# Second chunk pair decoded among the attention's last tiles, three products of the first slot behind its transposes, and the last slot and last token tiles reordered

## The chip, the cores and the metric

The kernel runs on one core of a Trainium2 chip. The metric is the device time of one execution in microseconds (us). Engines: TensorE (PE, with its weight loads as PEld), VectorE (DVE), ScalarE (ACT), GpSimd (POOL) and SyncE (SP), whose queue issues nearly all transfers.

## The reference

Three stages follow one another; everything is float32.

```python
scores = (q @ k.T) / sqrt(64) ; decay = cum[:, None] - cum[None, :]   # cum = cumsum(log(clip(f, 1e-4, 1)))
attn = softmax(where(causal, -1e9, scores + decay))                   # 4 batches, 8 heads, 576 tokens, 64 wide
x = (attn @ v)  as [2304 tokens, 512]
h = x @ w_in0  ; x = (h - tanh(h)) @ w_out0      # w_in 512 x 2048, w_out 2048 x 512
h = x @ w_in1  ; out = (h * sigmoid(h)) @ w_out1
```

## The kernel before, in words

**Precision.** Every float32 operand of a product is split in a high and a low part of the TensorE's faster 32-bit type, and each product is three matmuls: high x high, high x low, low x high. The split is a cast (ScalarE) and a subtraction (VectorE). The weights of the two feed-forward layers come as 64-bit words and are decoded on the chip: scale (ScalarE), shift, exponent, low, join (VectorE), then hi (ScalarE) and lo (VectorE). The function `wjob` issues one such step.

**Attention.** `attention` walks through 16 pairs of heads (NP) with 9 score tiles each (NTILE), so N = 144 tiles in all. One step of its loop issues, for tile n, the scores, transposes and values that are due (`later`, `run`), the copies out of PSUM (`evac`), the exponential of tile n - 1 (`expo`), the row minimum of tile n (`least`) and, every third step, the sums and the normalisation (GpSimd) of three tiles. `ahead` holds other work that is issued at the end of a step, by its number relative to N: `at(n - N, ...)`. Transposes have three PSUM tiles (ps_t), the scores four PSUM banks (ps_s), which become the product banks (ps_h) from step N on.

**Feed-forward units.** The hidden columns of a layer are cut into 16 chunks, two of them a pair (q); two pairs form a set. A unit u is (layer, set, block of 768 tokens); there are 24 and each has two slots (j = 0, 1), one for each pair of the set, so NSL = 48 slots. In a slot the first product (x with w_in) is done by a seven-product scheme (`product`, numbered 1 to 7) on blocks of half the width: operands 4 to 7 are made from differences of token blocks (`xtemp`, then `xmake`: cast on ScalarE, subtraction on VectorE, a spill to memory by SP), weights from sums and differences (`sum`). VectorE adds each product from its PSUM bank to half tiles hs (line 379); ScalarE copies product 1. `bend` applies tanh or silu, `high` and `low` split the result, and `project` (line 314) multiplies a half (h) of the tokens' hidden values with w_out.

**Order.** The whole order is written by hand (`tc.manual_schedule`): each engine's queue runs in the order in which the program issues, and a queue whose first instruction waits holds all behind it. `slot_steps` is a generator: a slot is a list of pieces, P for a product and G for one call of `project`; after each piece the items of `xplan` (operands of the next unit) and a share of `fills` (decoding) are issued. The G of slot sl are the projections from number n0 = 8 (sl - 1) - 6 on, so they lag behind their hidden values, and slot 0 has none that does anything. `rest` issues the split of the second half that the slot left over.

Before the change, the steps N - 1 to N + 7 hold the differences and operands of unit 0, steps N + 8 to N + 16 scale to sums of the w_in of pair 1 (`jobs(1, 0, ...)`), and the parts hi and lo of it are fills of slot 0, as is scale to join of w_out of pair 1. Its hi and lo are fills of slot 1, the lo in the last piece; the first projection that needs them is the third of slot 2, number 4 (the projections 0 to 3 belong to pair 0).

**The end.** `halves` lists the projections: per unit, half h, pair j, chunk i, and token group g. In layer 1 the group g = 0 has two tiles of 128 tokens (six matmuls of 512 columns), g = 1 one (three). The last projection of each group ends in an add into an output tile `ob` (line 334) and its transfer (line 336):

```python
ob = wtmp.tile([P, 2, DM], F32, tag="wb", name=f"ob{u}_{h}_{g}")
ob = ob[:, 0:2 - g]
nc.vector.tensor_tensor(ob.rearrange("p t (k w) -> p k t w", w=256), acc, total, ALU.add)
t0 += 256 * g
nc.sync.dma_start(out=out[t0:t0 + P * (2 - g), :].rearrange("(t p) d -> p t d", p=P), in_=ob)
```

The pool wtmp has one buffer for each of its tags wa, wb and ws; wa and wb are also the intermediate tiles of the decoding. The accumulators (ps_a) have two buffers.

Of the kernel before, what the change touches and what calls it, by code (L numbers as in the profile page):

```python
# [7 lines left out]
F32 = mybir.dt.float32  # L8
# [6 lines left out]
P = 128  # L15
# [24 lines left out]
def forgetting_attention_two_ffn(  # L40
# [160 lines left out]
    def jobs(q, m, *lists):  # L201
        return [(q, m) + j for js in lists for j in js] if q < 2 * NPR else []

    fills, late = {}, set()
    for s in range(2 * NSET):
# [11 lines left out]
            fills.setdefault(k + d, []).extend(js)  # L217
        late.add(k + 7)
        fills.setdefault(k + 7, []).extend(jobs(o, 1, LAST))
    fills[0] = jobs(1, 0, HILO) + jobs(1, 1, [("scale",)], PRE)  # L220
    fills[1] = jobs(1, 1, LAST)

    def fill(j):
# [43 lines left out]
    def xat(sl, p, fn, *a):  # L267
        xplan.setdefault((sl, p), []).append((fn, a))
# [3 lines left out]
    for u, (l, s, b) in enumerate(units):  # L272
        if u == 0:
            continue
        if s == 0:
            xat(2 * u - 2, 5, xtemp, l, b, 1)
            xat(2 * u - 2, 6, xtemp, l, b, 2)
            for p, i in ((2, 1), (4, 6), (6, 2)):
                xat(2 * u - 1, p, xmake, u, i)
            xat(2 * u - 1, 7, xtemp, l, b, 4)  # L280
            xat(2 * u - 1, 11, xmake, u, 5)
            xat(2 * u - 1, 12, xtemp, l, b, 3)
            xat(2 * u - 1, 13, xmake, u, 7)
            xat(2 * u, 0, xmake, u, 4)
            xat(2 * u, 2, xmake, u, 3)
        else:
            for i, p in PIECE.items():
                xat(2 * u - 1, p, xload, u, i)

    halves = [(u, h, q, i, g) for u in range(len(units)) for h in range(2) for q in range(2)  # L290
              for i in (1, 0) for g in range(2)]
    gfree, gt, accs, hs = list(range(4)), {}, {}, {}

    def project(n):

        u, h, j, i, g = halves[n]
        l, s, b = units[u]
        gh, gl, slot = gt[u, j, h]
        woh, wol = (w[:, i] for w in wtiles[2 * (u // NB) + j, 1])
        first, last = j == 0 and i == 1, j == 1 and i == 0  # L300
        if first:
            accs[u, h, g] = pools["ps_a"].tile([P, 2, 512], F32, tag="a", name=f"a{u}_{h}_{g}")
        acc = accs[u, h, g]
        ks = range(2) if l == 0 or g == 0 else range(1)
        for k in ks:
            js = slice((2 * g + k) * P, (2 * g + k) * P + P)
            if l == 0:
                terms = ((woh[:, js], gh[:, i]), (woh[:, js], gl[:, i]), (wol[:, js], gh[:, i]))
                dst = acc[:, k, 0:TH]
            else:  # L310
                terms = ((gh[:, i, js], woh), (gh[:, i, js], wol), (gl[:, i, js], woh))
                dst = acc[:, k]
            for r, (w, m) in enumerate(terms):
                nc.tensor.matmul(dst, w, m, start=first and r == 0, stop=last and r == 2)  # L314
        if g == 1 and i == 0:
            gfree.append(slot)
        if not last:
            return
        del accs[u, h, g]
        t0 = TB * b + TH * h  # L320
        if l == 0:
            total, acc = x[:, 2 * g:2 * g + 2, t0:t0 + TH], acc[:, :, 0:TH]
        else:
            total = x[:, 2 * h:2 * h + 2, TB * b + 512 * g:TB * b + 512 * g + (512, 256)[g]]
            total = total.rearrange("p k (t w) -> p k t w", w=256)
            acc = acc[:, 0:2 - g].rearrange("p t (k w) -> p k t w", w=256)
        if s == 0:
            nc.scalar.copy(total, acc)  # L328
        elif l == 0 or s + 1 < NSET:
            nc.vector.tensor_tensor(total, acc, total, ALU.add)  # L330
        else:
            ob = wtmp.tile([P, 2, DM], F32, tag="wb", name=f"ob{u}_{h}_{g}")
            ob = ob[:, 0:2 - g]
            nc.vector.tensor_tensor(ob.rearrange("p t (k w) -> p k t w", w=256), acc, total, ALU.add)  # L334
            t0 += 256 * g
            nc.sync.dma_start(out=out[t0:t0 + P * (2 - g), :].rearrange("(t p) d -> p t d", p=P), in_=ob)
# [12 lines left out]
    def half_tile(u, j, h):  # L349
        hs[h] = pools["hp"].tile([P, 2, TH], F32, tag=f"h{h}", name=f"hs{u}_{j}_{h}")  # L350
        return hs[h]
# [26 lines left out]
    def add(to, p, s):  # L378
        nc.vector.tensor_tensor(to, p, s, ALU.add)  # L379

    def slot_steps(sl):

        u, j = divmod(sl, 2)
        pieces = "P1 G P6 G P2 G G P7 G P5 G P4 G P3 G".split()
        n0 = 8 * (sl - 1) - 6
        todo = list(fills.get(sl, []))
        hooks = [4, 5, 6, 7, 11, 12, 14] if sl in late else [1, 2, 3, 4, 5, 6, 7, 11, 12, 14]
        share = {p: (len(todo) * k // len(hooks), len(todo) * (k + 1) // len(hooks)) for k, p in enumerate(hooks)}
        g = 0
        for p, what in enumerate(pieces):  # L390
            if what == "G":
                if n0 + g >= 0:
                    project(n0 + g)
                g += 1
            else:
                i = int(what[1])
                dst = product(u, j, i)
                if i == 1:
                    nc.scalar.copy(half_tile(u, j, 0)[:, 1], dst)
                    rest()  # L400
                elif i == 6:
                    add(half_tile(u, j, 1)[:, 0], dst, hs[0][:, 1])
                elif i == 2:
                    add(hs[0][:, 1], dst, hs[0][:, 1])
                elif i == 7:
                    add(hs[0][:, 0], dst, hs[1][:, 0])
                elif i == 5:
                    add(hs[1][:, 1], dst, hs[1][:, 0])
                    add(hs[1][:, 0], dst, hs[0][:, 0])
                elif i == 4:  # L410
                    add(hs[0][:, 0], dst, hs[0][:, 0])
                    bend(u, j, 0)
                else:
                    add(hs[1][:, 1], dst, hs[1][:, 1])
                    high(u, j, 0)
                    low(u, j, 0)
                    bend(u, j, 1)
                    left.extend([(high, (u, j, 1)), (low, (u, j, 1))])
            for fn, a in xplan.get((sl, p), []):
                fn(*a)  # L420
            for job in todo[slice(*share.get(p, (0, 0)))]:
                fill(job)
            yield

    def attention():
        with ExitStack() as actx:


# [316 lines left out]

            def open_early():
                early.close()
                open_pools(("ps_h", 4), xb=1)

            ahead = {-12: [(open_earlier,)], 0: [(open_early,)]}  # L750

            def at(n, *item):
                ahead.setdefault(n, []).append(item)
# [10 lines left out]
                at(NTILE * (4 + k // 3) + (1, 3, 5)[k % 3] - N, wjob, *job)  # L764
            for n, i in ((-11, 1), (-8, 2)):
                at(n, xmake, 0, i, nc.gpsimd)
            for n, k in ((-1, 1), (0, 2), (2, 4), (4, 3)):
                at(n, xtemp, 0, 0, k)
            for n, i in ((1, 6), (3, 5), (5, 7), (6, 4), (7, 3)):
                at(n, xmake, 0, i)  # L770
            for k, job in enumerate(jobs(1, 0, [("scale",)], PRE, SUMS)):
                at(8 + k, fill, job)
            for n in range(N + 2 * NTILE):
                if n % NTILE == 0:
                    run(n, scores)
                    run(n, transposes)
                    run(n, values)
                else:
                    run(n, transposes)
                    run(n, values)  # L780
                    run(n, scores)
                if n < NTILE - 1:
                    busy(kqs[0][:, 0], 2)
                run(n, evac)
                if has(n - 1):
                    expo(n - 1)
                run(n, collect)
                if n % 3 == 2 and has(n - 5):
                    guard(n - 5)
                if has(n):  # L790
                    least(tiles[n])
                if n % 3 == 2 and has(n - 5):
                    normalise(n - 5)
                run(n, load_kq, load_v, split, place_last, place_dec, place_dec_last)
                for fn, *a in ahead.get(n - N, []):
                    fn(*a)
        open_pools(("ps_a", 2), hp=1, tp=1, gp=1, wp1=1, wp2=1)
        wpool.update({1: pools["wp1"], 2: pools["wp2"]})

    with tc.manual_schedule():  # L800
        attention()
        for sl in range(NSL):
            for _ in slot_steps(sl):
                pass
        rest()
        for n in range(8 * (NSL - 2) + 2, len(halves)):
            project(n)
# [39 lines left out]
```

## Time and profile before

| | |
|---|---|
| median of 3 runs | 976.05 us (975.76 to 976.42) |
| profiled execution, its own time | 972.9 us |
| its span, first to last instruction | 971.1 us |
| mean granted TensorE clock | 0.989 |
| busy in the span: PE, PEld, DVE, ACT, POOL | 96%, 87%, 76%, 45%, 17% |
| moved by DMA | 188.86 MB, mean 194 GB/s |

The attention ends near 180 us (its last values product starts at 177.49); from there on slots follow each other. GpSimd is busy in the attention alone. Rows of a timeline or of the chain begin with the start and the duration in us; in brackets stands how long the engine was idle before, and what ended that.

### The profile page before, as it was taken

The numbers are of one execution on the slowest core, as the hardware profiler recorded it, in microseconds if no ns is written. First come the engines' busy times: TensorE is split into PE (matmuls) and PEld (weight loads), VectorE is DVE, ScalarE is ACT, GpSimd is POOL, SyncE is SP. The second block draws the span as 40 slices with busy tenths as digits, with TensorE's granted clock in tenths as the row PEclk, the third lists the DMA queues.
The fourth block names the chain that finished last, engine by engine and source line by source line (L and its number), as shares of the span: only waits on it lengthen the run. The fifth ranks groups of instructions, "written<-read, shape, count | busy, mean of one in ns | idle before, by whom it ended". The sixth has DMA issues, their size and how long they took to land.

```text
span 971.1 us, 14858 instructions
## 1 busy us (share of the span) xinstructions
PE 935.5 (96%) x5496; PEld 848.0 (87%) x5496; DVE 740.0 (76%) x1338; ACT 436.4 (45%) x782; POOL 160.5 (17%) x242
## 2 busy tenths in 40 slices
PE   8999999779999999999999989899999999999996
PEld 6777776669999999999999989798898989899884
DVE  7788887899888887888788988785676677765442
ACT  6788888454554333332423354554432334231210
POOL 8999998100000000000000000000000000000000
PEclk9999999899999999999999999999999999999998
DMA  5443343545558564866467345474865477435711
GB/s 163 144 139 121 128 154 122 206 186 222 225 224 312 189 224 138 308 245 207 154 251 271 141 169 234 167 269 166 295 236 191 178 250 271 154 135 189 271 62 68
DMA packets 45800, 188.86 MB, mean 194 GB/s; under 512 B 9440, under 2 KB 9440, under 8 KB 45696
## 3 DMA queue, kind: packets, MB, share of 16 engines
q1 hardware_dynamic: 45720, 187.90, 53.6%
q8 instruction: 43, 0.70, 0.3%
q14 instruction: 29, 0.24, 0.1%
q10 hardware_dynamic: 8, 0.02, 0.0%
HBM read 148.44 MB, written 38.34 MB: 192 GB/s over the span
## 4 chain that ended last, share of the span: by engine, by line
PE 82%; DVE 10%; ACT 3%; issue 2%; POOL 1%; DMA 1%; POOLq 0%; DVEq 0%; ACTq 0%
PE a L314 35%; PE h L346 30%; PE t L594 5%; PE s L547 4%; PE out_t L650 4%; DVE hs L379 3%; PE s L539 2%; PE out_t L678 1%; DVE xt L242 1%; DVE xo L256 1%; ACT t L356 1%; DMA out<-ob 1%; DVE wl L194 1%; DVE t L358 1%; DVE ob L334 1%
## 5 line engine op out<-in xcount | busy, mean ns | idle before, releaser
L346 PE MATMUL h<-xo,wh 128*128 128x384 f32 x1344 | 345.9, 338 | 8.0 <-DVE hs L379 8.0
L346 PEld LDWEIGHTS h<-xo,wh 128*128 128x128 f32 x1344 | 247.8, 190 | 24.2 <-DVE hs L379 7.5
L379 DVE TENSOR_TENSOR hs<-h,hs 128x384 f32<-128x384 f32 x336 | 185.3, 553 | 84.7 <-PE h L346 80.3
L356 ACT ACTIVATE t<-hs 128x768 f32<-128x768 f32 x96 | 81.3, 847 | 355.3 <-DVE hs L379 355.3
L346 PE MATMUL h<-xo,wl 128*128 128x384 f32 x672 | 226.8, 337 | 0.0
L314 PE MATMUL a<-gh,wh 128*128 128x384 f32 x384 | 129.4, 337 | 4.5 <-DVE x L330 4.5
L314 PE MATMUL a<-gh,wl 128*128 128x384 f32 x384 | 129.4, 337 | 2.6 <-DVE wl L194 2.6
L314 PE MATMUL a<-gl,wh 128*128 128x384 f32 x384 | 129.3, 337 | 0.0
L346 PEld LDWEIGHTS h<-xo,wl 128*128 128x128 f32 x672 | 127.3, 189 | 0.0
L369 DVE TENSOR_TENSOR gl<-t,gh 128x768 fp32r<-128x768 f32 x96 | 91.5, 953 | 41.9 <-ACT gh L365 41.7
L314 PE MATMUL a<-wh,gh 128*128 128x512 f32 x288 | 112.8, 392 | 6.4 <-ACT x L328 3.5
L314 PE MATMUL a<-wh,gl 128*128 128x512 f32 x288 | 114.6, 398 | 0.0
L314 PE MATMUL a<-wl,gh 128*128 128x512 f32 x288 | 114.1, 396 | 0.0
L365 ACT CAST gh<-t 128x768 fp32r<-128x768 f32 x96 | 80.4, 837 | 29.5 <-DVE t L358 28.3
L568 ACT ACTIVATE p<-p,mn 128x128 f32<-128x128 f32 (+3 forms) x128 | 71.1, 557 | 14.7 <-DVE mn L560 12.7
L314 PEld LDWEIGHTS a<-gh,wh 128*128 128x128 f32 x384 | 72.5, 189 | 5.4 <-DVE x L330 5.4
L314 PEld LDWEIGHTS a<-gh,wl 128*128 128x128 f32 x384 | 72.7, 189 | 2.9 <-DVE wl L194 2.9
L560 DVE CUSTOM_DVE_ANT_0 p<-s,mask 128x128 f32<-128x128 f32 (+3 forms) x128 | 59.4, 480 | 20.0 <-PE s L547 20.0
L582 POOL TENSOR_SCALAR p<-p,sm 128x128 f32<-128x128 f32 (+3 forms) x128 | 71.8, 580 | 12.6 <-DVE sm L579 8.1
L314 PEld LDWEIGHTS a<-gl,wh 128*128 128x128 f32 x384 | 72.6, 189 | 0.2 <-DVE gl L369 0.2
L314 PEld LDWEIGHTS a<-wh,gh 128*128 128x128 f32 x288 | 54.2, 188 | 14.1 <-DVE ob L334 4.1
L358 DVE TENSOR_TENSOR t<-hs,t 128x768 f32<-128x768 f32 x48 | 46.0, 957 | 25.6 <-ACT t L356 23.6
(90 smaller groups left out, 1233.2 us busy)
## 6 DMA issues: line engine op xcount, KB each, us to landing
xo<-xd SPq DMA_DIRECT2D x126, 768.0 KB
xd<-xo SPq DMA_DIRECT2D x42, 768.0 KB
raw<-w_in SPq DMA_DIRECT2D x32, 512.0 KB
raw<-w_out SPq DMA_DIRECT2D x32, 512.0 KB
kqraw<-kq SPq DMA_DIRECT2D x16, 608.0 KB
vraw<-v SPq DMA_DIRECT2D x16, 320.0 KB
out<-ob SPq DMA_DIRECT2D x6, 512.0 KB
out<-ob SPq DMA_DIRECT2D x6, 256.0 KB
```

Of the source, the lines that this page charges most:

```text
L314: nc.tensor.matmul(dst, w, m, start=first and r == 0, stop=last and r == 2)
L346: nc.tensor.matmul(dst, w[:, ks], m[:, k], start=k == 0 and r == 0, stop=k == 1 and r == 2)
L356: nc.scalar.activation(t, hs[h], AF.Silu if l else AF.Tanh)
L358: nc.vector.tensor_tensor(t, hs[h], t, ALU.subtract)
L365: nc.scalar.copy(gh, hs[h])
L369: nc.vector.tensor_tensor(gl, hs[h], rd(gh), ALU.subtract)
L379: nc.vector.tensor_tensor(to, p, s, ALU.add)
L547: nc.tensor.matmul(s[:, h, c:c + n], a[half(h), q], b[half(h), 0:n], start=r == 0, stop=r == 3,)
L560: nc.vector.tensor_tensor_reduce(out=pt.rearrange("p (g c) -> p g c", g=2) if i == 4 else pt, in0=src, in1=m, op0=ALU.add, op1=ALU.min, sc ...
L568: nc.scalar.activation(pt, pt, AF.Exp, bias=mn, scale=-1.0, accum_out=sums[:, n // 3 % 5, n % 3, 0:1],)
L582: nc.gpsimd.tensor_scalar(pt, pt, sm[:, j:j + 1], 1.0, ALU.mult, ALU.mult)
L594: nc.tensor.transpose(t[:, k], pt[:, c * P:c * P + P], ident)
```

## The change

In the attention, the steps N - 3 to N + 3 get scale, shift, exponent, low and join of pair 1's w_in, one each at N - 3, N - 2, N - 1, N and N + 3; the sums follow at N + 6. The differences and the operands 6, 5, 7 of unit 0 move to steps N + 1 to N + 8. The generator of slot 0 is advanced within the attention, three pieces at the steps N + 3, N + 4 and N + 6: products 1, 2 and 6 of slot 0. The loop ends nine steps earlier; behind it hi and lo of pair 1's w_in are issued, with the operands 4 and 3 of unit 0 in between. In slot 0 product 1 is kept in the second half tile; the five decoding steps of pair 1's w_out stand behind products 7, 5, 4 and two empty G. Unit 1's two first differences move from slot 0 to slot 1, and its operand 1 is made one piece earlier.

At the end, slot 47 runs product 3 before its last two projections and issues the left-over split at once; the last eight projections run with all of g = 0 first; and output tiles of g = 1 take the tag wa.

```diff
@@ -217,7 +217,7 @@
             fills.setdefault(k + d, []).extend(js)
         late.add(k + 7)
         fills.setdefault(k + 7, []).extend(jobs(o, 1, LAST))
-    fills[0] = jobs(1, 0, HILO) + jobs(1, 1, [("scale",)], PRE)
+    fills[0] = jobs(1, 1, [("scale",)], PRE)
     fills[1] = jobs(1, 1, LAST)
 
     def fill(j):
@@ -273,9 +273,10 @@
         if u == 0:
             continue
         if s == 0:
-            xat(2 * u - 2, 5, xtemp, l, b, 1)
-            xat(2 * u - 2, 6, xtemp, l, b, 2)
-            for p, i in ((2, 1), (4, 6), (6, 2)):
+            early = u == 1
+            xat(2 * u - 2 + early, 5 - 3 * early, xtemp, l, b, 1)
+            xat(2 * u - 2 + early, 6 - 3 * early, xtemp, l, b, 2)
+            for p, i in ((2 - early, 1), (4, 6), (6, 2)):
                 xat(2 * u - 1, p, xmake, u, i)
             xat(2 * u - 1, 7, xtemp, l, b, 4)
             xat(2 * u - 1, 11, xmake, u, 5)
@@ -289,6 +290,7 @@
 
     halves = [(u, h, q, i, g) for u in range(len(units)) for h in range(2) for q in range(2)
               for i in (1, 0) for g in range(2)]
+    halves[-8:] = sorted(halves[-8:], key=lambda t: t[4])
     gfree, gt, accs, hs = list(range(4)), {}, {}, {}
 
     def project(n):
@@ -312,7 +314,7 @@
                 dst = acc[:, k]
             for r, (w, m) in enumerate(terms):
                 nc.tensor.matmul(dst, w, m, start=first and r == 0, stop=last and r == 2)
-        if g == 1 and i == 0:
+        if g == 1 and i == 0 and (u, h) != (len(units) - 1, 1):
             gfree.append(slot)
         if not last:
             return
@@ -329,7 +331,7 @@
         elif l == 0 or s + 1 < NSET:
             nc.vector.tensor_tensor(total, acc, total, ALU.add)
         else:
-            ob = wtmp.tile([P, 2, DM], F32, tag="wb", name=f"ob{u}_{h}_{g}")
+            ob = wtmp.tile([P, 2, DM], F32, tag=("wb", "wa")[g], name=f"ob{u}_{h}_{g}")
             ob = ob[:, 0:2 - g]
             nc.vector.tensor_tensor(ob.rearrange("p t (k w) -> p k t w", w=256), acc, total, ALU.add)
             t0 += 256 * g
@@ -382,10 +384,16 @@
 
         u, j = divmod(sl, 2)
         pieces = "P1 G P6 G P2 G G P7 G P5 G P4 G P3 G".split()
+        if sl == 0:
+            pieces = "P1 P2 P6 G G G G P7 G P5 G P4 G P3 G".split()
+        elif sl == NSL - 1:
+            pieces = "P1 G P6 G P2 G G P7 G P5 G P4 P3 G G".split()
         n0 = 8 * (sl - 1) - 6
         todo = list(fills.get(sl, []))
         hooks = [4, 5, 6, 7, 11, 12, 14] if sl in late else [1, 2, 3, 4, 5, 6, 7, 11, 12, 14]
         share = {p: (len(todo) * k // len(hooks), len(todo) * (k + 1) // len(hooks)) for k, p in enumerate(hooks)}
+        if sl == 0:
+            share = {p: (k, k + 1) for k, p in enumerate((7, 9, 10, 11, 12))}
         g = 0
         for p, what in enumerate(pieces):
             if what == "G":
@@ -396,12 +404,16 @@
                 i = int(what[1])
                 dst = product(u, j, i)
                 if i == 1:
-                    nc.scalar.copy(half_tile(u, j, 0)[:, 1], dst)
+                    half_tile(u, j, 0)
+                    p1 = (half_tile(u, j, 1) if sl == 0 else hs[0])[:, 1]
+                    nc.scalar.copy(p1, dst)
                     rest()
                 elif i == 6:
-                    add(half_tile(u, j, 1)[:, 0], dst, hs[0][:, 1])
+                    if sl:
+                        half_tile(u, j, 1)
+                    add(hs[1][:, 0], dst, p1)
                 elif i == 2:
-                    add(hs[0][:, 1], dst, hs[0][:, 1])
+                    add(hs[0][:, 1], dst, p1)
                 elif i == 7:
                     add(hs[0][:, 0], dst, hs[1][:, 0])
                 elif i == 5:
@@ -416,13 +428,15 @@
                     low(u, j, 0)
                     bend(u, j, 1)
                     left.extend([(high, (u, j, 1)), (low, (u, j, 1))])
+                    if sl == NSL - 1:
+                        rest()
             for fn, a in xplan.get((sl, p), []):
                 fn(*a)
             for job in todo[slice(*share.get(p, (0, 0)))]:
                 fill(job)
             yield
 
-    def attention():
+    def attention(first):
         with ExitStack() as actx:
 
 
@@ -745,7 +759,7 @@
 
             def open_early():
                 early.close()
-                open_pools(("ps_h", 4), xb=1)
+                open_pools(("ps_h", 4), xb=1, hp=1)
 
             ahead = {-12: [(open_earlier,)], 0: [(open_early,)]}
 
@@ -764,13 +778,18 @@
                 at(NTILE * (4 + k // 3) + (1, 3, 5)[k % 3] - N, wjob, *job)
             for n, i in ((-11, 1), (-8, 2)):
                 at(n, xmake, 0, i, nc.gpsimd)
-            for n, k in ((-1, 1), (0, 2), (2, 4), (4, 3)):
+            pre = jobs(1, 0, [("scale",)], PRE)
+            for n, job in zip((-3, -2, -1, 0, 3), pre):
+                at(n, fill, job)
+            for n, k in ((1, 1), (1, 2), (4, 4), (7, 3)):
                 at(n, xtemp, 0, 0, k)
-            for n, i in ((1, 6), (3, 5), (5, 7), (6, 4), (7, 3)):
+            for n, i in ((2, 6), (5, 5), (8, 7)):
                 at(n, xmake, 0, i)
-            for k, job in enumerate(jobs(1, 0, [("scale",)], PRE, SUMS)):
-                at(8 + k, fill, job)
-            for n in range(N + 2 * NTILE):
+            for job in jobs(1, 0, SUMS):
+                at(6, fill, job)
+            for n in (3, 4, 6):
+                at(n, next, first)
+            for n in range(N + NTILE):
                 if n % NTILE == 0:
                     run(n, scores)
                     run(n, transposes)
@@ -794,13 +813,18 @@
                 run(n, load_kq, load_v, split, place_last, place_dec, place_dec_last)
                 for fn, *a in ahead.get(n - N, []):
                     fn(*a)
-        open_pools(("ps_a", 2), hp=1, tp=1, gp=1, wp1=1, wp2=1)
+        open_pools(("ps_a", 2), tp=1, gp=1, wp1=1, wp2=1)
         wpool.update({1: pools["wp1"], 2: pools["wp2"]})
 
     with tc.manual_schedule():
-        attention()
-        for sl in range(NSL):
-            for _ in slot_steps(sl):
+        slots = [slot_steps(sl) for sl in range(NSL)]
+        attention(slots[0])
+        for (q, m, *what), i in zip(jobs(1, 0, HILO), (4, None, 3, None)):
+            wjob(q, m, *what)
+            if i:
+                xmake(0, i)
+        for slot in slots:
+            for _ in slot:
                 pass
         rest()
         for n in range(8 * (NSL - 2) + 2, len(halves)):
```

## Rows read from the trace of the kernel before

**Rows 1.** Page, parts 1 and 5: busy time, count, mean ns, idle before.

```profile
PE 935.5 (96%) x5496; PEld 848.0 (87%) x5496; DVE 740.0 (76%) x1338; ACT 436.4 (45%) x782; POOL 160.5 (17%) x242
...
L346 PE MATMUL h<-xo,wh 128*128 128x384 f32 x1344 | 345.9, 338 | 8.0 <-DVE hs L379 8.0
```

**Rows 2.** Busy times by stretch: us, PE, PEld, DVE, ACT, POOL, clock, DMA, GB/s.

```profile
174.00:176.00 2.00, 1.77 (x8) 1.43 (x9) 1.19 (x3) 1.00 (x2) 1.59 (x2) 0.57 0.75 310
181.00:218.20 37.20, 26.54 (x127) 24.34 (x125) 33.46 (x46) 17.59 (x24) 0.00 (x0) 0.91 0.47 180
222.00:538.00 316.00, 316.00 (x1824) 316.00 (x1824) 265.61 (x371) 122.30 (x154) 0.00 (x0) 1.00 0.61 225
...
922.00:953.00 31.00, 30.62 (x149) 26.70 (x147) 14.81 (x21) 6.79 (x9) 0.00 (x0) 1.00 0.14 51
953.00:971.10 18.10, 8.77 (x36) 6.60 (x36) 2.81 (x4) 0.00 (x0) 0.00 (x0) 0.86 0.23 87
```

**Rows 3.** Chain that ended last, 951 us to the end: start, us, what.

```profile
951.98 1.24 DVE ob L334
...
953.23 2.80 DMA out<-ob
...
956.90 6.43 PE a L314 x27
...
964.61 2.79 DMA out<-ob
...
967.52 0.69 DVE ob L334
```

**Rows 4.** Timeline of PE in the last slots and behind them.

```profile
914.09 0.50 PE L314 MATMUL a<-wh,gh 128*128 128x512 f32 x1 [0.34 <-DVE ob L334]
...
953.26 0.50 PE L314 MATMUL a<-wh,gh 128*128 128x512 f32 x1 [0.64 <-DVE ob L334]
```

**Rows 5.** Timeline of DVE, 165 to 218 us, the instructions that waited longest and four others.

```profile
165.74 0.76 DVE L560 CUSTOM_DVE_ANT_0 pt<-s,mask 128x576 f32<-128x576 f32 x1 [0.68 <-PE t L594]
...
170.09 0.96 DVE L256 TENSOR_TENSOR xo<-xt,xo 128x768 fp32r<-128x768 f32 x1 [0.94 <-ACT xo L255]
...
182.08 0.69 DVE L161 TENSOR_SCALAR wa<-raw 128x1024 uint32<-128x1024 uint32 x1 [2.05 <-ACT raw L157]
...
183.54 1.23 DVE L168 SCALAR_TENSOR_TENSOR wb<-raw,wb 128x1024 f32<-128x1024 uint32 x1
184.80 1.22 DVE L176 TENSOR_TENSOR ws<-wa,wb 128x1024 f32<-128x1024 f32 x1
...
196.17 0.96 DVE L358 TENSOR_TENSOR t<-hs,t 128x768 f32<-128x768 f32 x1 [0.91 <-ACT t L356]
...
210.90 0.96 DVE L358 TENSOR_TENSOR t<-hs,t 128x768 f32<-128x768 f32 x1 [0.97 <-ACT t L356]
...
216.90 1.22 DVE L194 TENSOR_TENSOR wl<-wa,wh 128x1024 fp32r<-128x1024 f32 x1
```

**Rows 6.** Timeline of PE, 181 to 218 us.

```profile
181.48 0.51 PE L346 MATMUL h<-xo,wh 128*128 128x384 f32 x2
...
182.00 0.51 PE L346 MATMUL h<-xo,wh 128*128 128x384 f32 x2
...
189.25 0.84 PE L346 MATMUL h<-xo,wh 128*128 128x384 f32 x2
...
190.21 0.84 PE L346 MATMUL h<-xo,wh 128*128 128x384 f32 x2
...
218.17 0.44 PE L314 MATMUL a<-gh,wl 128*128 128x384 f32 x1 [2.63 <-DVE wl L194]
```

**Rows 7.** Timeline of POOL in the attention's last tiles.

```profile
161.00 1.38 POOL L582 TENSOR_SCALAR p<-p,sm 128x512 f32<-128x512 f32 x2
...
171.52 2.66 POOL L582 TENSOR_SCALAR p<-p,sm 128x512 f32<-128x512 f32 x2 [1.91 <-PE out_t L650]
```

**Rows 8.** Timeline of ACT in slot 0.

```profile
187.64 1.05 ACT L192 CAST wh<-ws 128x1024 fp32r<-128x1024 f32 x1 [0.70 <-DVE ws L181]
```

## The prediction

> **What bounds the kernel now.** The page comes first: TensorE is busy for 96% of the span [rows 1]. An average over stages with different limits says little, so the second view cuts the span into stretches [rows 2]. From 222 to 538 us TensorE is busy for 316.00 of 316.00 us at full clock; there nothing but less TensorE work could help. From 181 to 218.2 it is busy for 26.54 of 37.20 while VectorE is busy for 33.46, and in the last 18.1 us it is busy for 8.77. The change can act only in these two stretches and in a gap near 914 us. The chain of waits shows what ends last at the end of the kernel [rows 3], and the timelines of the engines, read by the idle time in brackets, show what each waited for [rows 4 to 6].
>
> **The last token tiles: removes two waits.** Now the last unit's four output tiles (two per half of the tokens) all take tag wb, which has one buffer. In the chain of the end, the add of the first half's g = 1 cannot start until the transfer of its g = 0 has landed: add 1.24, transfer 2.80, add 0.69; only then is the accumulator free for which TensorE waits. At the very end the same follows once more: transfer 2.79, add 0.69 from 967.52, and its own transfer until the span ends at 971.1, 2.89 after the add [rows 3, 4]. In the changed kernel g = 1 has its own buffer (wa, whose last weight use lies some slots back), and the second half runs its four g = 0 products (24 matmuls) before its four g = 1 (12). Step by step: the first matmul of that half still waits for the add of the first half's g = 0 and starts at 953.26 as now [rows 4]. The 27 matmuls of the chain took 6.43, with 0.39 for the last one's length that is (6.43 - 0.39) / 26 = 0.232 from start to start, so 36 of them end at 953.26 + 35 x 0.232 + 0.39 = 961.8. The g = 0 add (1.24) and its transfer (2.8) start some 2.6 us earlier, beside the last 12 matmuls. The first half's g = 1 add follows directly on its g = 0 add, at about 953.2 to 953.9, and its transfer has landed by 957, long before wa is wanted again and before TensorE wants the second accumulator at 953.26 + 24 x 0.232 = 958.8. What is late next is the last add: 961.8 + 0.7 = 962.5, and 2.89 behind it the span would end at 965.4, 5.7 us earlier. The tail can hardly give less than 5: if the last two transfers, issued some 2 us apart, got in each other's way, by less than the 0.7 that the smaller one's add takes, I estimate.
>
> The same single buffer makes VectorE wait in each of the last slots; TensorE felt it once, for 0.34 us at 914.09 [rows 4]. That wait goes: 0.3 us. In the last slot one projection moves behind product 3. The same matmuls run; TensorE is full there (30.62 of 31.00 us busy from 922 to 953 [rows 2]), and the left-over split is issued earlier, hidden behind 27 matmuls either way: nothing.
>
> **The front: what decides it.** TensorE's idle time between 181 and 218 is not its own. The last wait of that stretch is 2.63 us at 218.17 for the low part of the pair 1 output weights, a VectorE instruction that starts at 216.90 and lasts 1.22 [rows 5, 6]. From there TensorE is full until 538. So the front is worth just what moves that one instruction, and its queue is VectorE's, in order. The program puts the same VectorE work ahead of it in both kernels: decode of pair 1, all operands of unit 0, unit 1's operands 1, 6, 2, 5, 7, the adds of slots 0 and 1. Therefore I count VectorE's idle time from 165 to 218 before and after.
>
> Before, the waits are seven: 0.68 (165.74), 0.94 (170.09), two that add up to 1.46, 2.05 (182.08, for ScalarE's scaling), 0.91 and, the last, 0.97 (for the activation function), 7.0 us [rows 5]. Besides, shift, exponent, low, join and sums stand directly behind one another at 182 to 187 and can't overlap, some 0.1 each; of this about 0.3 goes.
>
> After, in queue order. The shift (0.69) of step N-2 falls into the 0.68 wait: that wait is gone. Exponent (as long as the shift), low (1.23) and join (1.22) [rows 5] replace operand work that moves back. In their place new waits arise, since a value and its consumer now stand next to each other:
> - operand 6 right behind the second difference: the ScalarE round trip, 0.94 as at 170.09, less some 0.45 of softmax sums in between: 0.5
> - the add of product 2: TensorE reaches product 2 only behind transposes that wait for GpSimd's last normalisation (two tiles, 171.52 + 2.66 = 174.2 [rows 7]). Then 8 transposes (I estimate 1.0, and 0.7 for a PSUM tile that is not copied out yet) and product 2 itself, six matmuls at 0.52 per three = 1.04 [rows 6]: ready at 176.9. VectorE ends the sums at about 171.4 as now, then come the 0.5, operand 6 (0.96), join (1.22), a difference (as long as operand 6) and two copies (0.9, I estimate): 175.9. So 1.0
> - operand 7 right behind the last difference: 0.94; operand 4, whose cast stands behind a weight cast: 0.55
> - the activation in slot 0: 0.91; the split of the second half, whose wait the join used to cover: 0.93
> - slot 1: operand 6 right behind the second difference, now made in slot 1, one add between: 0.47; operand 2, whose cast stands behind a weight cast of 1.05 [rows 8]: 0.8; the activation: 0.97
>
> Together 7.1. The front gains 7.0 + 0.3 - 7.1 = 0.2 us, within its error. The three products that TensorE now runs among the transposes (3 x 1.04 = 3.1 us) are saved on an engine that then waits longer for the same instruction, about 5 us rather than 2.63 at the second pair's first projection. Scale and sums and the spills of the operands (SP) move with their steps; the load of pair 2's input weights is issued some 15 us earlier, behind the low of step N, and nothing behind it on SP is awaited before unit 1. Scale on ScalarE (1.1 in place of nothing at step N-3) delays two PSUM copies by some 0.2, inside waits.
>
> **The unknown cost** is the wait for product 2, as no row shows a product among transposes. From below: zero, if TensorE has it by 175.9, which gives 1.0 more. From above: the granted clock was 0.57 from 174 to 176 [rows 2], close to the lower level of 1.2 GHz, after the gaps of the attention's end. At that level three matmuls take 0.96 (189.25 to 190.21) in place of 0.52 [rows 6]: products 1 and 2 cost 0.88 more each, the transposes as much again: 2.6 more. I take 1.0, since real products replace idle time there.
>
> One rule speaks against the place of the decode. GpSimd's two 512-wide tiles took 1.38 at 161.00, with VectorE idle, and 2.66 at 171.52, beside VectorE's differences and splits [rows 7]. The Trainium skill (SBUF — State Buffer, section Who interferes with whom) says that GpSimd and a VectorE instruction with two SBUF inputs, or one in a two-port mode, share a port pair, and that whoever comes second blocks until the other is done. By that rule the trace agrees, and join, 1.22 long where a split is 0.96 [rows 5], could hold a normalisation for 0.3 longer than now; exponent and low could do so for 1.2, which the front would then lose. As differences already ran there, I leave the sum as it is.
>
> **How it stands to the runs.** The profiled execution took 972.9 (span 971.1, 1.8 around it); the runs' median is 976.05. Changes are taken off the median: 5.7 + 0.3 + 0.2 = 6.2, so 969.8.
>
> **Rivals.**
> 1. The front gains what TensorE no longer has to do, 3.1 us: 976.05 - 5.7 - 0.3 - 3.1 = 967.0. For it: the waits in 186 to 204 are all TensorE waiting for an add in a bank, 8.0 us in all [rows 1], and three adds are made early. Against it: the instruction that ends the last wait is not among them.
> 2. The front loses 2.6: the products sit in TensorE's queue ahead of the transposes, at the lower clock, and VectorE's adds of them ahead of the copies of the attention: 976.05 - 6.0 + 2.6 = 972.6. For it the clock of 0.57; against it that TensorE has less idle time there.
> 3. Slower than before: TensorE stays at the lower clock from the end of the attention up to the second pair's first projection. 18 products and projections lie there, 1.92 each at that level, 34.6 in all; from 183.8, when operand 7 is ready, that ends at 218.4 even if it never waits, and with the 8.0 of waits for adds [rows 1] at 226.4, 8.2 behind 218.17. Less the 6.0 of the end that is 978.3. It decides from the point where these waits add up to over 6 instead of lying beside slower matmuls. Against it: with as many gaps the granted clock was 0.91 on the mean of that stretch [rows 2].
> 4. The output part does not do what it says: the last g = 1 add waits for a transfer all the same (2.8): 972.6.
>
> **How the numbers follow.** Forecast 0.60, with a range of its own of 968.4 to 971.2 (the wait for product 2 from 0 to 2.4); rival 1 0.15; rivals 2 and 4 together 0.20; rival 3 0.05. Range: 966.6 to 972.9, which leaves out rival 3, the far part of rival 2 and a front better than 3.5. About 0.2% (1.95 us) can be told from no change here: faster than 974.1 hold the forecast, rival 1 and nearly all of 2 and 4: 0.91; within 0.04; slower 0.05.
>
> **What would show it.** Tail: no wait for a transfer ahead of any output add, 36 matmuls in one run from about 953 - 0.5, and 2.9 us from the last add to the end. Front: the pair 1 low split of output weights still ends TensorE's last wait, at 218.17 - 0.2, with 4 to 6 us of idle time before it; the add of product 2 waits some 1 us for TensorE; clock near 1.00 around 174 to 178. It is wrong if that split moves by over 1.5 us, or if an output add waits for a transfer.

## The result, and the profile after

The changed kernel takes 968.05 us in the median of 7 runs, beside 976.42 for the kernel before; the ratio is 0.9912 (95% interval 0.9883 to 0.9940), which is 5.9 to 11.4 us less. Run once more on another occasion it took 969.56 beside 975.65, ratio 0.9940 (0.9918 to 0.9961), 3.8 to 8.0 less. Forecast were 969.8 and 6.2 less.

The profiled execution took 970.84 us, its span 969.0: only 2.1 less than the span before. A table by stretch tells where the rest of the gain went in this one execution. The table answers to [rows 2]; its columns are the stretch and its length, busy times of PE, PEld, DVE, ACT and POOL, the granted clock, the DMA share and GB/s.

```profile
172.00:174.00 2.00, 1.65 (x12) 1.69 (x13) 2.00 (x3) 0.80 (x3) 2.00 (x3) 1.00 0.73 297
174.00:176.00 2.00, 1.38 (x12) 1.10 (x11) 2.00 (x3) 1.69 (x4) 1.33 (x1) 1.00 0.85 344
181.00:218.20 37.20, 23.82 (x120) 20.55 (x116) 31.34 (x41) 18.89 (x25) 0.00 (x0) 0.94 0.48 191
222.00:538.00 316.00, 316.00 (x1820) 316.00 (x1818) 264.76 (x370) 122.33 (x154) 0.00 (x0) 1.00 0.61 225
538.00:618.00 80.00, 72.36 (x371) 68.83 (x371) 68.90 (x96) 35.97 (x46) 0.00 (x0) 0.93 0.45 178
...
906.00:922.00 16.00, 16.00 (x82) 14.41 (x81) 7.66 (x12) 3.74 (x5) 0.00 (x0) 1.00 0.96 331
922.00:953.00 31.00, 31.00 (x154) 27.58 (x153) 14.92 (x23) 7.01 (x9) 0.00 (x0) 1.00 0.20 78
```

TensorE is full from 222 to 538 as before. In the first slots (181 to 218.2) it does 2.7 us less work, since three products now lie ahead of them, and the stretch is no shorter. The clock from 174 to 176 is 1.00 where it was 0.57 (on which more below). From 538 to 618, where the layer changes, the clock is 0.93. The wait near 914 is gone.

The end is where the gain is. The chain of waits answers to [rows 3] (start, us, what):

```profile
948.12 7.54 PE a L316 x33
955.66 0.02 issue
955.69 1.24 DVE ob L336
956.92 0.04 issue
956.97 8.47 PE a L316 x36
965.43 0.02 issue
965.46 0.69 DVE ob L336
```

No transfer stands in it any more. The 36 matmuls of the last half run in one piece, 8.47 us long (8.5 was worked out), and the last half takes 969.0 - 956.97 = 12.03 us from its first matmul to the end, where it took 971.1 - 953.26 = 17.84 [rows 4]: 5.8 us less. VectorE's timeline shows the output adds; those of g = 1 (512 columns) that waited for a transfer do so no longer:

```profile
928.59 1.23 DVE L336 TENSOR_TENSOR ob<-a,x 128x1024 f32<-128x1024 f32 x1 [0.83 <-PE a L316]
...
930.79 0.68 DVE L336 TENSOR_TENSOR ob<-a,x 128x512 f32<-128x512 f32 x1
...
955.69 1.82 DVE L336 TENSOR_TENSOR ob<-a,x 128x1024 f32<-128x1024 f32 x2 [3.65 <-PE a L316]
962.74 1.23 DVE L336 TENSOR_TENSOR ob<-a,x 128x1024 f32<-128x1024 f32 x1 [5.23 <-PE a L316]
965.46 0.69 DVE L336 TENSOR_TENSOR ob<-a,x 128x512 f32<-128x512 f32 x1 [1.49 <-PE a L316]
```

Beside the first trace of the kernel before, the front gave nothing by its waits (a second trace of that kernel, in the last experiment, says more). VectorE's timeline from 164 to 218, with every instruction that waited and, last, the one that decides [rows 5]:

```profile
167.50 1.48 DVE L168 SCALAR_TENSOR_TENSOR wb<-raw,wb 128x1024 f32<-128x1024 uint32 x1
...
171.96 1.02 DVE L256 TENSOR_TENSOR xo<-xt,xo 128x768 fp32r<-128x768 f32 x1 [0.66 <-ACT xo L255]
...
177.13 0.56 DVE L381 TENSOR_TENSOR hs<-h,hs 128x384 f32<-128x384 f32 x1 [0.99 <-ACT xo L255]
...
183.04 0.96 DVE L256 TENSOR_TENSOR xo<-xt,xo 128x768 fp32r<-128x768 f32 x1 [0.90 <-ACT xo L255]
184.51 0.96 DVE L256 TENSOR_TENSOR xo<-xt,xo 128x768 fp32r<-128x768 f32 x1 [0.51 <-ACT xo L255]
...
192.58 0.96 DVE L360 TENSOR_TENSOR t<-hs,t 128x768 f32<-128x768 f32 x1 [0.91 <-ACT t L358]
...
199.17 0.96 DVE L371 TENSOR_TENSOR gl<-t,gh 128x768 fp32r<-128x768 f32 x1 [0.90 <-ACT gh L367]
...
204.27 0.96 DVE L256 TENSOR_TENSOR xo<-xt,xo 128x768 fp32r<-128x768 f32 x1 [0.48 <-ACT xo L255]
205.96 0.96 DVE L256 TENSOR_TENSOR xo<-x,xo 128x768 fp32r<-128x768 f32 x1 [0.73 <-ACT xo L255]
...
210.95 0.96 DVE L360 TENSOR_TENSOR t<-hs,t 128x768 f32<-128x768 f32 x1 [0.97 <-ACT t L358]
...
216.95 1.22 DVE L194 TENSOR_TENSOR wl<-wa,wh 128x1024 fp32r<-128x1024 f32 x1
```

Nine waits, 7.05 us in all, where the seven of the kernel before came to 7.0. The add at 177.13 is that of product 2: the profile names ScalarE's cast, but that had ended at 176.50, and the matmuls of product 2 ended just ahead of the add. The low part of pair 1's output weights starts at 216.95 (216.90 before), and TensorE waits for it until 218.23 (218.17):

```profile
215.16 0.45 PE L316 MATMUL a<-gl,wh 128*128 128x384 f32 x1 [1.88 <-DVE gl L371]
218.23 0.69 PE L316 MATMUL a<-gh,wl 128*128 128x384 f32 x1 [2.62 <-DVE wl L194]
```

From there to the first matmul of the last half it took 956.97 - 218.23 = 738.7 us, before 953.26 - 218.17 = 735.1. These 3.7 us more, and 5.8 less at the end, make the 2.1 of the spans. The program's instructions in that stretch are the same but for order at its end; what differs in the rows is the clock. The stretches behind the last wait of the first slots and behind the two waits of the layer's change, in the kernel before:

```profile
216.00:234.00 18.00, 15.83 (x82) 15.83 (x83) 16.11 (x22) 9.00 (x13) 0.00 (x0) 0.91 0.45 171
570.00:592.00 22.00, 18.49 (x105) 17.72 (x104) 20.42 (x29) 9.02 (x11) 0.00 (x0) 1.00 0.58 225
605.00:627.00 22.00, 18.55 (x84) 16.28 (x83) 18.36 (x29) 10.43 (x13) 0.00 (x0) 0.92 0.41 153
```

and in the changed one:

```profile
216.00:234.00 18.00, 15.77 (x76) 15.78 (x77) 15.14 (x21) 8.09 (x11) 0.00 (x0) 0.81 0.38 148
570.00:592.00 22.00, 18.50 (x92) 18.18 (x91) 19.11 (x27) 9.59 (x12) 0.00 (x0) 0.84 0.50 197
605.00:627.00 22.00, 19.17 (x81) 16.71 (x80) 17.50 (x27) 11.72 (x15) 0.00 (x0) 0.84 0.36 148
```

A second trace of the changed kernel (below) has 0.81, 0.92 and 0.84 there and takes 736.8 us for the same work, so some 2 of the 3.7 us are a difference between executions and not one of the programs. The last experiment takes up the rest.

### The profile page after: what moved, and what is told of

It reads as the page before. It is cut to its first block, busy times and chain, and to the rows that moved or that the text cites. A ratio compares the mean times of both kernels' runs of the same rounds, so it can differ in the third digit from the quotient of the medians.

```text
span 969.0 us, 14850 instructions
## 1 busy us (share of the span) xinstructions
PE 936.4 (97%) x5496; PEld 849.8 (88%) x5496; DVE 741.0 (76%) x1338; ACT 437.5 (45%) x782; POOL 161.3 (17%) x242
## 4 chain that ended last, share of the span: by engine, by line
PE 82%; DVE 10%; ACT 3%; issue 3%; POOL 1%; DMA 1%; ACTq 0%; DVEq 0%; POOLq 0%
PE a L316 37%; PE h L348 31%; PE t L608 4%; PE s L561 4%; PE out_t L664 4%; DVE hs L381 2%; PE s L553 2%; DVE xo L256 1%; DVE xt L242 1%; DVE wl L194 1%; ACT t L358 1%; ACT xo L255 1%; DVE t L360 1%; POOL p L596 1%; ACT wh L192 0%
## 5 line engine op out<-in xcount | busy, mean ns | idle before, releaser
L316 PEld LDWEIGHTS a<-wh,gl 128*128 128x128 f32 x288 | 54.4, 189 | 11.8
```

## The experiments

Theory A is that of the prediction: the end gives about 6 us, the front nothing, since one VectorE instruction decides it. Rival B: the front gives 2 to 3 us, as the gain of the first comparison (8.4 by the medians) is more than 6. Rival C: what TensorE has left to do decides the front.

**The end alone.** The kernel before with all edits of the end and none of the front:

```diff
+    halves[-8:] = sorted(halves[-8:], key=lambda t: t[4])
-            ob = wtmp.tile([P, 2, DM], F32, tag="wb", name=f"ob{u}_{h}_{g}")
+            ob = wtmp.tile([P, 2, DM], F32, tag=("wb", "wa")[g], name=f"ob{u}_{h}_{g}")
...
```

> The kernel before with the edits of the end alone (order of the last eight projections, tag wa for g = 1, last slot's pieces). Theory A (the end gives all of the gain, the front nothing): from the first matmul of the last half to the end of the span 12.0 us in place of 17.8, the wait of 0.34 near 914 gone; 6.1 us less than before in the timed runs, ratio about 0.9938, the same as the whole change. Rival B (the front gives the 2 to 3 us by which the timed gain of 8.4 exceeds 6.1): the same 6.1 here, but the whole change then stays 2 to 3 us ahead of it.

Ratio 0.9906 (0.9871 to 0.9940). Last half to end: 965.0 - 952.86 = 12.14 us; last wait of the first slots at 218.33; no wait near 914. By the medians it is 9.9 us less where 6.1 were expected; the expected ratio, 0.9938, still lies in the interval. The end alone is level with the whole change.

**The front alone.** The changed kernel with those edits taken out.

> The changed kernel with the edits of the end undone. Theory A: the last wait of TensorE in the first slots (for the low part of pair 1's output weights) ends at 218.2 as in both kernels, and the time is that of before within 0.5 us, apart from what the clock does. Rival B: 2 to 3 us less than before, ratio 0.997 to 0.998.

Ratio 0.9975 (0.9952 to 0.9997). In the trace the waits are as A has them: 218.21, last half to end 970.2 - 952.39 = 17.81. But the timed runs are 2.4 us ahead of before, more than A's 0.5, with an interval that ends just short of no change. By itself this speaks for B. The fastest runs of that occasion, all at a granted clock of 0.990 to 0.992, speak against it: 972.32 and 972.33 for the kernel before, 971.87 twice for the front alone, 966.38 and 966.40 for the end alone. There the front gives 0.5 and the end 5.9, as A has it; what remains of the 2.4 stands in runs at a lower clock.

**The whole once more.** No edit.

> The changed kernel once more, beside the kernel before on one chip. Theory A (the end gives 6, the front nothing by its waits): 6 us less than before at the same granted clock, ratio 0.992 to 0.994, the same as the end alone (0.9906 with an interval of 0.9871 to 0.994). Rival B (the front gives 2 to 3 besides): ahead of the end alone by 2 to 3, ratio 0.988 to 0.990.

Ratio 0.9940 (0.9918 to 0.9961), 5.9 us less (6.1 by the medians). It is not ahead of the end alone, as B wants, but behind it, with overlapping intervals. In the trace the first slots' last wait ends at 218.94 and the last half takes 967.8 - 955.71 = 12.09. With both occasions together B has no support but the run of the front alone; a gain of the front of up to some 2 us in the timed runs is neither shown nor excluded.

**The buffer alone, the order alone.** The kernel before with the tag line, and with the sorted `halves` (and the condition on the free slot that goes with them), each by itself.

> The kernel before with the second output buffer alone (tag wa for g = 1). From the first matmul of the last half to the end of the span before 17.8, whole change 12.0. Worked out: 36 matmuls without a break, 8.5, then the add of g = 0 (1.24, started three matmuls earlier), the add of g = 1 (0.69) behind it and its transfer (2.9): 12.6 to 13.2, so about 4.9 of the 5.8 us come from the buffer.

> The kernel before with the order of the last eight projections alone (all of g = 0 first), both output tiles still in one buffer. Worked out: the first half's g = 1 add still waits for a transfer, now beside TensorE's 24 matmuls; the last g = 0 add waits for the transfer of that tile until about 959.7, its own transfer lands at 963.8, the last add at 964.5, the end at 967.4: 14.1 from the first matmul of the last half to the end in place of 17.8, so 3.7 of the 5.8 us.

The buffer alone: ratio 0.9949 (0.9931 to 0.9968), last half to end 968.1 - 954.76 = 13.34. The order alone: 0.9961 (0.9943 to 0.9978), 967.2 - 953.63 = 13.57. The two gains do not add up: the buffer alone gives 4.5, the order alone 4.3, both 5.8. Each takes away most of the same wait. Both missed their expectations by a little: the buffer's 12.6 to 13.2 and the order's 14.1. With the buffer alone VectorE's two last adds follow each other:

```profile
962.59 1.82 DVE L334 TENSOR_TENSOR ob<-a,x 128x1024 f32<-128x1024 f32 x2 [7.29 <-PE a L314]
```

They end at 964.4, and the span 3.7 us later, not 2.9 as in the whole change (965.46 + 0.69 = 966.15 to 969.0): as I read it, and no run shows it by itself, two transfers issued 0.6 apart hold each other up by 0.8, which the order avoids by issuing the larger one 2.2 ahead. With the order alone VectorE still waits for a transfer at the end, now with TensorE at work (until 962.1) beside the first of these waits and half of the last:

```profile
956.51 0.69 DVE L335 TENSOR_TENSOR ob<-a,x 128x512 f32<-128x512 f32 x1 [2.94 <-DMA out<-ob]
959.42 1.23 DVE L335 TENSOR_TENSOR ob<-a,x 128x1024 f32<-128x1024 f32 x1 [2.22 <-PE a L315]
963.60 0.69 DVE L335 TENSOR_TENSOR ob<-a,x 128x512 f32<-128x512 f32 x1 [2.95 <-DMA out<-ob]
```

**No products among the transposes.**

```diff
-            for n in (3, 4, 6):
-                at(n, next, first)
```

> The changed kernel without the three products among the attention's transposes: all of slot 0 runs behind the attention, the decoding stays early. Theory A (one VectorE instruction, the low part of pair 1's output weights, decides the front): VectorE no longer waits 0.99 for product 2, so that instruction comes 0.5 to 1.0 earlier than 216.95 and the kernel is not slower than the changed one. Rival C (TensorE's work decides the front): TensorE has 3.1 us more to do after the attention and the mark at 218.2 and the end come some 3 us later.

Ratio 0.9911 (0.9883 to 0.9940). TensorE goes on at 217.66 in place of 218.23, though it has three products more to do after the attention; C wanted some 221:

```profile
214.59 0.44 PE L316 MATMUL a<-gl,wh 128*128 128x384 f32 x1 [1.88 <-DVE gl L371]
217.66 0.69 PE L316 MATMUL a<-gh,wl 128*128 128x384 f32 x1 [2.63 <-DVE wl L194]
```

The end of this wait (the mark, from here on) differs by as much between executions of one program (218.23 and 218.94 for the changed kernel), so the gain is better counted from an instruction that all these kernels share, the row minimum of the attention that waits 2.67 us for its scores. In the changed kernel it is

```profile
162.94 0.69 DVE L574 CUSTOM_DVE_ANT_0 p<-s,mask 128x512 f32<-128x512 f32 x1 [2.67 <-PE s L561]
```

and in this one it starts at 163.28. From its start to the mark it takes 55.29 us in the changed kernel, 55.25 in its second trace and 54.38 here. So the early products cost 0.9 us, about the wait of 0.99 for product 2, and saved none.

**The differences of unit 1 back in slot 0.**

```diff
-            early = u == 1
+            early = 0
```

> The changed kernel with the two first differences of unit 1 back in slot 0 and its operand 1 back at its old piece. Theory A (VectorE's queue decides, and its two waits of 0.48 and 0.73 in slot 1 arise because a difference now stands directly ahead of its consumer): these two waits go, the low part of pair 1's output weights starts at about 215.8 in place of 216.95, and TensorE goes on 1.2 us earlier. Rival C (TensorE's work decides): no change.

Ratio 0.9920 (0.9899 to 0.9940). The waits of 0.48 and 0.73 are gone from VectorE's timeline, and TensorE goes on 1.4 us earlier (1.2 expected):

```profile
213.77 0.44 PE L316 MATMUL a<-gl,wh 128*128 128x384 f32 x1 [1.07 <-DVE gl L371]
216.84 0.57 PE L316 MATMUL a<-gh,wl 128*128 128x384 f32 x1 [2.62 <-DVE wl L194]
```

**The deciding instruction moved.**

```diff
+        if sl == 1:
+            share = {5: (0, 1), 9: (1, 2)}
```

> The changed kernel with one instruction moved: the low part of pair 1's output weights is issued behind product 5 of slot 1 instead of at the slot's end. Theory A: TensorE then waits only for the split of the hidden values, which comes 1.14 later than now and ends at about 216.3, so that it goes on 1.9 us earlier than 218.23 and the kernel ends 1.9 us earlier (1 to 3 with the clock). Rival C: TensorE's own work decides, the instruction is not what it waits for in sum, and the end moves by less than 0.5.

Ratio 0.9884 (0.9855 to 0.9914), the lowest of the three edits of the changed kernel, though their intervals overlap; the traces tell them apart. TensorE's last wait is for the split of the hidden values and ends at 216.16, 2.1 us earlier (1.9 expected):

```profile
213.82 0.44 PE L316 MATMUL a<-gh,wh 128*128 128x384 f32 x1 [0.78 <-ACT gh L367]
216.16 0.44 PE L316 MATMUL a<-gl,wh 128*128 128x384 f32 x1 [1.89 <-DVE gl L371]
```

**All three.** The last three edits together.

> The changed kernel with three edits together: no products among the transposes, unit 1's first differences back in slot 0, the low part of pair 1's output weights behind product 5 of slot 1. Each alone brought TensorE's last wait of the first slots forward, by 0.6, 1.4 and 2.1 us in the profiles. Theory A (VectorE's queue decides): they add up, that wait ends near 214.2 in place of 218.23, and the kernel is 4 us ahead of the changed one, ratio 0.988 to 0.991 to before. Rival C (TensorE's own work takes over on the way): under 2.5 us.

963.17 us, ratio 0.9869 (0.9844 to 0.9894), a little better than the 0.988 to 0.991 expected and ahead of both kernels: the interval lies wholly below that of the whole change run once more (0.9918 to 0.9961). It overlaps a little with that of the first comparison (0.9883 to 0.9940), but four of its five runs (962.40 to 963.96) lie below all thirteen of the changed kernel (965.81 to 970.90). TensorE's last wait ends 4.6 us earlier than in the changed kernel, beside 0.9 + 1.4 + 2.2 = 4.5 for the three edits counted from the shared row minimum, so they add up, as A has it. The wait is also shorter, and the clock behind it stays at its upper level (1.00 from 216 to 234, where the changed kernel has 0.81):

```profile
213.61 0.44 PE L316 MATMUL a<-gl,wh 128*128 128x384 f32 x1 [1.54 <-DVE gl L371]
```

**The kernel before, a second trace.**

> The kernel before once more, for a second trace of the same program. If the spread between runs of one kernel is the granted clock behind the long waits (218, 575 and 611 us), the waits of this trace stand within 0.8 us of the first up to 218, and the time from 218 to the last half differs by as much as the mean clock in those three stretches does. If the spread has another source, the clock there is the same and the time differs all the same.

The last wait of the first slots ends at 217.61, within the expected 0.8 us of the first trace:

```profile
217.61 0.69 PE L314 MATMUL a<-gh,wl 128*128 128x384 f32 x1 [2.63 <-DVE wl L194]
```

From there to the last half it takes 952.88 - 217.61 = 735.3 us, in the first trace 735.1; the clock is 0.91, 0.92 and 0.92 in the three stretches where it was 0.91, 1.00 and 0.92. So 1.8 us of lower clock in the second stretch cost 0.2 here, and the expectation that time follows the clock by its whole difference failed. That it costs less because part of the lower clock falls where TensorE waits anyway is my reading and not shown.

That time does follow the clock shows when the twelve traces of all kernels are put side by side, the clock being the mean of the 20 us behind each of the two waits of the layer's change. Between the two waits it takes 35.5 us at 1.00 (three traces), 36.0 at 0.91 to 0.92 (five) and 36.9 to 37.1 at 0.86 to 0.87 (four). From the second wait to the last half it takes 341.0 at 1.00 (one), 341.9 to 342.6 at 0.91 to 0.93 (five) and 343.1 to 343.2 at 0.84 to 0.85 (six). The 3.7 us that the changed kernel's first trace is behind make 1.35 ahead of the first of these waits (clock behind 218 us 0.86, before 0.91), 1.62 between the two and 0.68 behind them, each at a lower clock. The kernel before with the buffer alone has the lower steps too (36.9 and 343.2), so the change is not needed for them; whether it makes them more frequent is not shown.

In the 17 timed runs of before that stood beside the first four experiments, the mean granted clock went from 0.980 to 0.990; at 0.990 both runs took 972.3, at 0.980 they took 978.2 to 980.3. The order is not strict: the three slowest runs, 980.95 to 981.19, had 0.983.

This trace also has another clock among the attention's last transposes, 1.00 from 172 to 181 us, where the first trace of before has 0.81. Its row minimum starts at 162.96, as in the first trace, so the mark stands 54.6 us behind it. The kernel with the buffer alone has 54.6 as well, at 1.00; the three traces with the old front at 0.81 have 55.2 to 55.3. The changed front has 55.2 to 55.3 in its three traces, all at 1.00. At the same clock, then, the changed front is 0.6 us later than the old one.

## Why the prediction was right

- **The end, 5.7:** 5.8 measured, by the mechanism named. The 36 matmuls took 8.47 (8.5), the first half's adds follow each other (955.69, 1.82 for both), and 2.85 lie behind the last add (2.89). The last two transfers, some 2 us apart, show no delay; 0.6 apart they ended 0.8 later, where I had taken 0.7 as the most.
- **The wait at 914, 0.3:** gone.
- **The front, 0.2:** -0.05 by the two first traces, and -0.6 at the same clock. The seven waits of 7.0 us from which I started stand in a trace at the lower clock; in the second trace of that kernel, at 1.00, the waits in brackets come to 6.3, and the mark is 0.6 earlier. So the term for the waits before was too large by this much, and that the first traces agree is luck; beside the 6.2 in all it is small. The list of new waits held term by term, forecast beside measured: 0.5 and 0.66, 1.0 and 0.99, 0.94 and 0.90, 0.55 and 0.51, 0.91 and 0.91, 0.93 and 0.90, 0.47 and 0.48, 0.8 and 0.73, 0.97 and 0.97; 7.1 and 7.05. The term that was a little off is the 0.3 for instructions no longer behind one another: the low at step N took 1.48 instead of 1.23 [rows 5], and the difference at 174.97 took 1.16 where most take 0.95.
- **The wait for product 2, 1.0:** 0.99, in part by luck. I had its transposes wait for GpSimd until 174.2; GpSimd's two tiles were done at 173.55, and the transposes started without a wait at 174.11, behind product 1 in TensorE's own queue. The wait for a PSUM tile, 0.7 in my estimate, was 0.62:

```profile
174.11 0.60 PE L608 MATMUL t<-ident,p 128*128 128x128 f32 x4
175.33 0.66 PE L608 MATMUL t<-ident,p 128*128 128x128 f32 x4 [0.62 <-ACT ptf L653]
```

- **The port rule:** GpSimd's second group of three tiles, in whose time the exponent, the low and a difference fall, took 3.64 in place of 2.85, and the third pair 2.06 in place of 2.66 [rows 7]. In GpSimd's timeline after:

```profile
166.58 3.64 POOL L596 TENSOR_SCALAR p<-p,sm 128x256 f32<-128x256 f32 x3 [2.33 <-DVE sm L593]
171.49 2.06 POOL L596 TENSOR_SCALAR p<-p,sm 128x512 f32<-128x512 f32 x2 [1.27 <-DVE sm L593]
```

  The Trainium skill (SBUF — State Buffer, section Who interferes with whom) has a GpSimd instruction and a VectorE one with two inputs in SBUF block each other: the second waits until the first is done. The trace agrees in so far as instructions of both engines get longer; that one is held for the other's whole length, no row shows. The price of the low was 0.25 on VectorE, well under the 1.2 that I had named as the bound. No run separates the two engines.
- **Rival 1** (TensorE's work, 3.1): refuted by the kernel without early products, which was 0.6 earlier at the mark (0.9 from the shared row minimum), and by the two kernels that gained with TensorE's work unchanged.
- **Rivals 2 and 3** (lower clock): the clock was 1.00 among the transposes (0.57 before), and the mark moved by only 0.06. In the kernel before, the lower clock among the transposes cost 0.6 at the mark, not the 2.6 that rival 2 takes for a kernel with products there. The upper clock is no merit of the products: from 172 to 181 the clock is 1.00 as well without them, and in the second trace of the kernel before, as the row of that trace shows:

```profile
172.00:181.00 9.00, 6.49 (x46) 4.19 (x45) 6.66 (x10) 5.85 (x10) 3.60 (x3) 1.00 0.76 306
```

  My reason for the value that I took (real products replace idle time) is therefore not borne out, though the value is.
- **Rival 4:** no output add waits for a transfer.
- **The range of the forecast itself:** 968.4 to 971.2 does not follow from its terms. With no wait for product 2 the sum gives 969.8 - 1.0 = 968.8, and with the 2.6 of the lower clock on top of the 1.0 it gives 972.4.
- **What I did not foresee** is that single executions of one kernel lie several us apart, 965.81 to 970.84 for the changed kernel and 972.65 to 981.65 for before; the first spread is wider than the 2.8 us of the forecast's own range. The forecast difference of 6.2 lies between the two measured ones, 8.6 and 5.9 by the ratios, and in both intervals. The first median, 968.05, lies below the forecast's own range and nearer to rival 1's 967.0 than to 969.8; the second, 969.56, lies in it. It is the traces, not the medians, that decide between the two.

## What to carry to other kernels

Where one engine waits for another, ask which single instruction ends its last wait, and count the idle time of the engine that issues it; here work taken from the waiting engine gained nothing, and one instruction moved in the other's queue gained 2.1 us. Before waits of one trace are added up, a second trace of the same program tells which of them belong to the clock of that execution. A value made directly ahead of its consumer costs an in-order queue a round trip to the other engine (0.5 to 1.0 us here); put other ready work between. At the end of a kernel, a one-buffer output tile put a transfer (2.8 us) on the path for each of the last two pairs of tiles; a second buffer or an order that puts the larger tiles first each took most of it away, and the two gains did not add up.

## What the runs showed of the hardware

- Two transfers of 512 and 256 KB issued 0.6 us apart ended 0.8 us later than the second alone behind its add (3.7 in place of 2.9); issued 2.2 us apart they did not. That the one held up the other was not measured by itself.
- The granted clock behind a wait of 2.8 to 3.5 us differs from execution to execution: at the same place of the same program the mean of 22 us was 1.00 in one trace and 0.92 in another, and in the changed kernel 0.84 and 0.92. The time to the same later matmul goes with it: behind the layer's change 341.0 us at 1.00 and 343.1 to 343.2 at 0.84 to 0.85.
